# The last q load, its cast and two store flushes moved a dozen letters forward in a hand-written plan (attention, then a token-mixing MLP, one core)

## The chip, the cores and the metric

The kernel runs on one core of a Trainium2 chip. Its engines are TensorE (PE in the profile, with its weight loads as PEld), VectorE (DVE), ScalarE (ACT), GpSimd (POOL) and SyncE (SP, which here only issues DMAs). Each has its own queue and works it off in order; they wait for each other with semaphores. The time is the device time of one execution in microseconds (us). The kernel before took 186.4 us, the median of three runs (185.95 to 187.24); a fourth execution was profiled.

## The reference

There are 8 batches, 12 heads, 448 positions and 64 elements a head. Attention with a sigmoid in place of the softmax gives x (8 x 448 x 768); a MLP then mixes the tokens of each batch with weights that are computed from x itself.

```python
scores = scale * np.matmul(q, k.transpose(0, 1, 3, 2)) - np.log(S)
attn = 1.0 / (1.0 + np.exp(-scores))
x = heads_side_by_side(np.matmul(attn, v))        # 8 x 448 x 768
wq, wk = x @ w_q, x @ w_k                         # 8 x 448 x 64
W_tok = (1 / sqrt(64)) * np.einsum('bsd,btd->bst', wq, wk)
mixed = np.einsum('bst,btd->bsd', W_tok, x)
out = np.maximum(mixed, 0.0) @ w_out
```

## The kernel before

**Tiles.** Work goes by quads: four heads of one batch, 24 quads in all (0 to 23), three to a batch. A quad has seven score steps, each of 64 key positions for four heads. Matmuls work on 64 x 64 quarters of the array, four side by side. PSUM's eight banks are used as four pairs (numbers 0 to 3); which pair a step takes is written out in a string of digits, and a step waits until whoever reads that pair has done so.

**The plan.** The order of all work is a string, PLAN, with a letter for each step; small and capital letters of a kind differ in the engine that copies the result out of PSUM. A loop (L828) walks it and issues each step's instructions to the queues, so the string fixes the order on every engine. The letters around the change:

- S: four score products (L316) into a pair of banks, then the sigmoid on ACT (L332), which frees the pair. S number n belongs to quad n // 7.
- P and p: four products of the sigmoid's result with v (L346). The seventh of a quad is followed by the copy of x out of PSUM, "xt" (L356), which frees the pair.
- c and d: DVE's transposes (L272) of a quad's q and k from its cast tile into the tile "qk" that S reads. They need the tile as GpSimd has arranged it.
- L and l: the wq/wk products of one batch (L406), six letters to a batch. Behind the sixth, DVE adds the two halves (L414, L415) and GpSimd copies wq into a second tile (L420); for the last batch, number 7, DVE does that copy, so GpSimd's last one is that of batch 6.
- N: the transposes of wk (L445, run as L124). x and X: transposes of x (L376). U: L458, the product "tmp" out of wkn and xn. M and m: mixing (L486), which reads the copied wq. O and o: a quarter of an output product (L590). The fourth copies the result to a tile o (L604) and puts a store on a list.
- D: flush(1) (L881, L523). It takes the oldest store off the list and issues its two DMAs on SP.

**Loads.** q, k and v are loaded on SP in a fixed order, ORDER (L703), into six buffers used in turn. pump_loads (L724) runs at every letter and issues the next load as soon as the load six before it has been cast in program order. Two loads have a further condition in BEHIND: `("q", 23): (2642, 2276)` says that the load is put into SP's queue only once more than 2642 products have been issued, and that, in the queue, it waits for product number 2276. pump (L768) runs right after and issues casts in ORDER's order, each as soon as its load has been issued and its target tile is free.

**The cast and the arrangement.** cast1 (L207) puts a quad's q and k, on GpSimd, into one bf16 tile (L212). Once both are there, arrange (L160) follows on GpSimd in the same breath: one copy to a swap tile (L167), two (L170) and two more (L173) that exchange blocks of 32 rows. So a q cast brings five more GpSimd instructions behind it.

Around the change the plan reads, in two pieces with the batch-6 L and l letters in the middle:

```text
... S O L S c l l L S L L S D o d O D S O N x O P S p c p d p D ...
```

Counting the products along it, the first L begins at product 2582, the c stands at 2590, the last L issues products 2610 to 2613 and with them GpSimd's wq copy. The first D comes at 2618, the second at 2642. The O that follows the next S is the first letter at which more than 2642 products have been issued (2646): there the load of q 23, its cast and its arrangement are issued. On GpSimd's queue they stand behind the wq copy. Five stores are on the list at the first L; the two that the two D letters take are output stores of 128 rows by 768 that L657 issues, two DMAs each.

Of the kernel before, what the change touches and what calls it, by code (L numbers as in the profile page):

```python
# [17 lines left out]
def kernel(  # L18
# [111 lines left out]
    def xt(u, j):  # L130
# [14 lines left out]
        "xDSPpPxSPpPDSuwcWwdSSMWOoSMSDwwOOSDxpPSPrPSmPpPDooNDSDSosoOz"  # L145
        "oSDDSxOOSUDpSDPPPDSPpcDSPoDODSSSodOoOSPMpSPPPSPPSwWwoScMSdOw"
        "wSSWOONSPMPcpSPPPPSSOodXSOSxoSoxSOppSpcUPSPpPSoOSdSxOOSPPPmp"
        "pPSPoSoMmOSOLScllLSLLSDodODSONxOPSpcpdpDPSPSPoOSoSOSOoSUSoSO"
        "SpPPpp1SoSOpSPOSOyppPMpPpplMlmlxlLlxOoONooUoOMmooOmooOoOOOOO"
        "oOOOOooOo"  # L150
    )
# [557 lines left out]
    )  # L709
    BEHIND = {("q", 23): (2642, 2276), ("v", 23): (2732, 2404)}  # L710
    BY = {"s": [], "v": []}
    for x in ORDER.split():
        if x[0] == ".":
# [10 lines left out]
    def pump_loads():  # L724
        while len(loaded) < len(ORDER):
            nm, n = ORDER[len(loaded)]
            if len(ring) >= 6 and ring[-6] not in cast:
                break
            emit, m = BEHIND.get((nm, n), (0, 0))
            if emit >= len(products):  # L730
# [204 lines left out]
```

## Time and profile before

| what | value |
|---|---|
| median of three runs | 186.4 us (185.95, 186.4, 187.24) |
| the profiled execution's own time | 186.12 us |
| its span, first to last instruction | 184.3 us |
| PE busy | 171.8 us (93% of the span) |
| ACT busy | 159.6 us (87%) |
| DVE busy | 134.7 us (73%) |
| GpSimd busy | 116.9 us (63%) |
| DMA | 48.50 MB, mean 263 GB/s |

The page's span is 1.8 us shorter than the execution's own time; that part lies before the first and after the last instruction. The shares are means over the whole span and say little on one place: the kernel has a start of some 30 us in which loads and casts set the pace, a long middle in which PE is nearly always busy, and an end in which only output products are left. How the parts hang together is read from the chain of waits (the chain that ended last, followed backwards) and from the timeline, which lists instructions in order of time: start, duration, engine, line, operation, and in brackets the idle time before it with what ended it. In the timeline, runs of equal instructions are merged ("x12") and a row of SP gives the time in which its queue was issuing DMAs.

### The profile page before, as it was taken

The page shows a single profiled execution, that of the slowest core. Times are in us where ns is not written, and L with a number is a line of the kernel's source. Part 1 is how long each engine was busy: PE and PEld are TensorE (multiplying, and loading weights), DVE is VectorE, ACT ScalarE, POOL GpSimd, SP SyncE. Part 2 cuts the span into 40 slices and gives each one's busy share as a digit, 9 for nine tenths or more (in the row PEclk, how much of TensorE's full clock was granted, in tenths as well). Part 3 has the DMA queues.
Part 4 walks back from the last instruction along what each step waited for, and adds up shares of the span by engine and source line. Part 5 has one row for each costly group of instructions (what it writes and reads, how often), then busy time and mean ns, then how long its engine had stood idle before and what let it go on. Part 6 is the DMA issues. An engine that isn't in the chain of part 4 may idle for free.

```text
span 184.3 us, 8238 instructions
## 1 busy us (share of the span) xinstructions
PE 171.8 (93%) x3533; PEld 113.1 (61%) x3534; DVE 134.7 (73%) x207; ACT 159.6 (87%) x207; POOL 116.9 (63%) x156
## 2 busy tenths in 40 slices
PE   7888889899999999999999999999999987999990
PEld 7545435444564555655555556546788886889970
DVE  2457699978998898988758886689786845695310
ACT  4699999999999999999999999889989896984330
POOL 1238787998899995699999919999993270000000
PEclk9999999999999999999999999999999999999999
DMA  5998999969998859999799999997875332442686
GB/s 175 343 386 266 347 377 402 377 215 320 377 396 331 285 193 273 323 320 365 264 240 321 343 305 305 294 403 275 263 212 175 92 88 65 111 92 71 145 219 170
DMA packets 24260, 48.50 MB, mean 263 GB/s; under 512 B 3872, under 2 KB 16416, under 8 KB 24224
## 3 DMA queue, kind: packets, MB, share of 16 engines
q1 hardware_dynamic: 24000, 47.69, 78.3%
q8 instruction: 27, 0.44, 0.9%
q10 hardware_dynamic: 224, 0.30, 0.5%
q14 instruction: 9, 0.07, 0.1%
HBM read 35.78 MB, written 11.01 MB: 254 GB/s over the span
## 4 chain that ended last, share of the span: by engine, by line
PE 78%; DVE 8%; ACT 6%; issue 3%; POOL 2%; DMA 2%; SPq 0%; DVEq 0%; ACTq 0%
PE banks L121 73%; ACT at L332 5%; PE banks L124 4%; DVE qk L252 2%; DVE xt L356 2%; DMA ld<-in_moe_w_k_dram 2%; DVE qk L265 1%; DVE mx L470 1%; POOL wqk L759 1%; POOL qk L212 1%; DVE k L222 1%; DVE xn L385 0%; DVE qk L272 0%; DVE wqk L430 0%; ACT qk L806 0%
## 5 line engine op out<-in xcount | busy, mean ns | idle before, releaser
L332 ACT ACTIVATE at<-banks 128x896 bf16<-128x896 f32 x168 | 141.3, 944 | 7.5 <-PE banks L121 6.9
L121 PE MATMUL banks<-qk 64*64 64x448 bf16 x672 | 61.1, 361 | 5.0 <-ACT at L332 2.5
L121 PE MATMUL banks<-wout,mx 64*64 64x384 bf16 (+2 forms) x816 | 65.4, 324 | 0.1
L212 POOL CAST qk<-ld 128x896 bf16<-128x896 f32 x38 | 44.7, 1194 | 8.4 <-issue 7.4
L121 PEld LDWEIGHTS <-mx 64*64 64x64 bf16 (+2 forms) x816 | 39.1, 105 | 16.4 <-issue 6.0
L121 PE MATMUL banks<-at,v 64*64 64x448 bf16 x672 | 46.8, 350 | 0.3 <-ACT at L332 0.2
L121 PEld LDWEIGHTS <-qk 64*64 64x64 bf16 x672 | 26.5, 105 | 27.0 <-issue 19.4
L356 DVE CAST xt<-banks 128x896 bf16<-128x896 f32 x23 | 24.9, 1084 | 7.7 <-PE banks L121 5.8
L121 PEld LDWEIGHTS <-v 64*64 64x64 bf16 x672 | 23.1, 106 | 6.1 <-issue 1.1
L470 DVE TENSOR_SCALAR mx<-banks 128x896 bf16<-128x896 f32 (+1 forms) x21 | 19.9, 956 | 5.8 <-PE banks L121 5.1
L222 POOL CAST v<-ld 128x896 bf16<-128x896 f32 x22 | 20.4, 934 | 1.2 <-DMA ld<-in_v_dram 0.9
L272 DVE STREAM_TRANSPOSE qk<-qk 128x448 f32<-128x448 f32 x26 | 16.0, 630 | 2.7 <-POOL qk L173 2.6
L385 DVE COPY xn<-banks 128x896 bf16<-128x896 bf16 x21 | 13.1, 624 | 3.8 <-PE banks L124 3.4
L252 DVE STREAM_TRANSPOSE qk<-qk 32x448 f32<-32x448 f32 x24 | 15.3, 636 | 0.6
L170 POOL COPY qk<-qk 32x448 uint32<-32x448 uint32 x26 | 14.4, 554 | 1.6
L173 POOL COPY qk<-swap 32x448 uint32<-32x448 uint32 x26 | 14.4, 554 | 1.5
L121 PE MATMUL banks<-xt,wqk 64*64 64x448 bf16 (+1 forms) x84 | 13.8, 353 | 0.2 <-ACT at L332 0.2
L651 DVE COPY o<-banks 128x384 f32<-128x384 f32 x17 | 9.4, 553 | 3.4 <-PE banks L121 3.0
L124 PEld LDWEIGHTS <-xt 64*64 64x64 bf16 (+1 forms) x588 | 9.8, 108 | 3.2 <-issue 1.8
L124 PE MATMUL banks<-ident,xt 64*64 64x64 bf16 (+1 forms) x588 | 10.4, 194 | 0.2
L121 PE MATMUL banks<-wqk,tmp 64*64 64x448 bf16 (+3 forms) x72 | 8.5, 291 | 0.0
L121 PE MATMUL banks<-wq,tmp 64*64 64x448 bf16 (+2 forms) x72 | 8.4, 292 | 0.0
(68 smaller groups left out, 136.7 us busy)
## 6 DMA issues: line engine op xcount, KB each, us to landing
ld<-in_q_dram SPq DMA_DIRECT2D x24, 448.0 KB, 5.8
ld<-in_v_dram SPq DMA_DIRECT2D x24, 448.0 KB, 5.7
ld<-in_k_dram SPq DMA_DIRECT2D x23, 448.0 KB, 5.5
out_dram<-o SPq DMA_DIRECT2D x38, 192.0 KB, 5.0
out_dram<-ld SPq DMA_DIRECT2D x14, 192.0 KB, 2.8
ld<-in_moe_w_out_dram SPq DMA_DIRECT2D x6, 384.0 KB, 5.1
wout<-wout SPq DMA_DIRECT2D x6, 192.0 KB, 5.7
out_dram<-o SPq DMA_DIRECT2D x4, 96.0 KB, 1.9
```

Source lines behind the costliest of these rows:

```text
L121: products.append(nc.tensor.matmul(*args, **kw))
L124: products.append(nc.tensor.transpose(*args, **kw))
L170: eng.tensor_copy(out=w[lo, 1], in_=w[hi, 0])
L173: eng.tensor_copy(out=w[hi, 0], in_=z[lo])
L212: COPY[e](out=f[:, :, "qk".index(nm)].rearrange("p e i d y -> p e y i d"), in_=ld.pop((nm, n)).rearrange("p (y i e d) -> p e y i d", y=2, ...
L222: COPY[e](out=t16.rearrange("p i b d -> p b i d"), in_=ld.pop((nm, n)).rearrange("p b (i d) -> p b i d", i=NI),)
L252: nc.vector.transpose(out=qk[n][other : other + 32, h].rearrange("p t i n -> p (t i n)").bitcast(F32), in_=w[own : own + 32, 1 - h],)
L272: nc.vector.transpose(out=qk[n][:, t].rearrange("p t i n -> p (t i n)").bitcast(F32), in_=w)
L332: nc.scalar.activation(dst, src, ACTF.Sigmoid, bias=attn_bias, scale=attn_scale)
L356: COPY[eng](out=xt(u, j), in_=ps)
L385: COPY[eng](out=xn, in_=ps)
L470: nc.vector.tensor_scalar(dst, ps, moe_scale, 0.0, ALU.mult, ALU.max)
```

## The change

The two letters D that stood behind the last L letters of batch 6 now stand in front of the c. The condition under which the load of q 23 is issued falls from "more than 2642 products" to "more than 2590 products"; the product that the load waits for in SP's queue, 2276, stays. With the new number the load is issued at the second l behind the c, where 2594 products have been issued, and the cast of q 23 with its arrangement at the same letter. On GpSimd's queue these six instructions now come ahead of the wq copy of batch 6, which is issued with the last L. No instruction is added or removed.

```diff
-        "pPSPoSoMmOSOLScllLSLLSDodODSONxOPSpcpdpDPSPSPoOSoSOSOoSUSoSO"
+        "pPSPoSoMmOSOLSDDcllLSLLSodOSONxOPSpcpdpDPSPSPoOSoSOSOoSUSoSO"
...
-    BEHIND = {("q", 23): (2642, 2276), ("v", 23): (2732, 2404)}
+    BEHIND = {("q", 23): (2590, 2276), ("v", 23): (2732, 2404)}
```

## The prediction

> **What bounds the kernel now.** I read the page's busy shares first, then the chain that ended last, then, at the one place where the chain leaves PE near the change, the timeline by engine. The busy shares and the granted clock:
>
> ```profile
> PE 171.8 (93%) x3533; PEld 113.1 (61%) x3534; DVE 134.7 (73%) x207; ACT 159.6 (87%) x207; POOL 116.9 (63%) x156
> PEclk9999999999999999999999999999999999999999
> ```
>
> PE is busy for 93% of the span at full clock, so over most of it only a PE pause is worth anything. The chain in order of time, late part:
>
> ```profile
> 146.89 4.73 PE banks L121 x106
> 151.62 0.03 DVEq L604
> 151.65 0.60 DVE qk L272
> 152.25 0.99 DVE xt L356
> 153.24 0.04 issue
> 153.28 7.71 PE banks L121 x186
> ...
> 166.46 13.48 PE banks L121 x310
> ```
>
> From 146.89 to the last output products near 179.95 the chain is on PE, but for one detour over DVE between 151.62 and 153.28: a transpose (L272), then the copy of x (L356). The timeline shows PE there:
>
> ```profile
> 148.85 0.41 PE L121 MATMUL banks<-at,v 64*64 64x448 bf16 x4
> ...
> 150.69 0.41 PE L121 MATMUL banks<-qk 64*64 64x448 bf16 x4
> 150.88 0.71 PE L121 MATMUL banks<-wout,mx 64*64 64x384 bf16 x12
> ...
> 153.28 0.38 PE L121 MATMUL banks<-qk 64*64 64x448 bf16 x4 [1.68 <-DVE xt L356]
> ```
>
> The products at 153.28 are score step S159. Its banks are pair 1, which held the x of quad 21 and comes free with the copy xt. That x was complete with the four v products at 148.85, so near 149.26. Why the copy came three microseconds later stands in DVE's rows:
>
> ```profile
> 147.58 0.95 DVE L604 COPY o<-banks 128x768 f32<-128x768 f32 x1
> 151.08 1.17 DVE L272 STREAM_TRANSPOSE qk<-qk 128x448 f32<-128x448 f32 x2 [2.55 <-POOL qk L173]
> 152.17 1.05 DVE L356 CAST xt<-banks 128x896 bf16<-128x896 f32 x1
> 153.15 0.94 DVE L604 COPY o<-banks 128x768 f32<-128x768 f32 x1
> ```
>
> DVE was free at 148.53 and stood 2.55 us at the two transposes of quad 23 (c, d), which stand ahead of xt in its queue and wait for GpSimd's last L173 copy. S159 doesn't need them: it belongs to quad 22. GpSimd's rows give the cause:
>
> ```profile
> 138.65 1.20 POOL L212 CAST qk<-ld 128x896 bf16<-128x896 f32 x1
> 146.15 0.56 POOL L420 COPY wq<-wqk 64x448 bf16<-64x448 bf16 x1 [6.31 <-ACT at L332]
> 146.77 1.20 POOL L212 CAST qk<-ld 128x896 bf16<-128x896 f32 x1
> 148.03 0.56 POOL L167 COPY swap<-qk 128x448 uint32<-128x448 uint32 x1
> 148.66 1.17 POOL L170 COPY qk<-qk 32x448 uint32<-32x448 uint32 x2
> 149.88 1.17 POOL L173 COPY qk<-swap 32x448 uint32<-32x448 uint32 x2
> ```
>
> After the cast of k 23 (138.65 to 139.85) GpSimd idles 6.31 us at the wq copy, which needs DVE's sum (L415). The page names ACT as the releaser; the row that fits is this one, ending at 145.99:
>
> ```profile
> 145.37 0.62 DVE L415 TENSOR_TENSOR wqk<-banks,wpart 128x448 bf16<-128x448 f32 x1
> ```
>
> Behind the copy stand the cast of q 23 and its arrangement, 146.77 to 151.05. So GpSimd's order, not its speed, makes the pause: it waits idle with work behind it.
>
> **The change part by part.** SP's queue and the load, in the views of SP and of the DMA issues:
>
> ```profile
> 127.00 4.73 SPq L657 DMA_DIRECT2D out_dram<-o  x6
> 132.50 0.33 SPq L190 DMA_DIRECT2D ld<-in_q_dram  x1
> 134.29 1.31 SPq L612 DMA_DIRECT2D out_dram<-o  x2
> ld<-in_q_dram SPq DMA_DIRECT2D x1, 448.0 KB, 4.6
> ```
>
> Six L657 DMAs are three stores: one forced out by the tile allocation at the O before the first L, and those of the two D. Then comes q 23's load. After the change the two D still take the same two stores (the list holds five there) and still stand ahead of the load. So SP's order doesn't change at all: 0 us. Were the D not moved, the load would pass two stores. The load is issued at 132.50 as before, and lands 4.6 us later, at 137.1.
>
> GpSimd: the cast of q 23 now follows that of k 23, 139.85. The load has been there for 2.75 us; the cast's tile is that of k 23, already being written. The five instructions with their gaps take what they took, 151.05 - 146.77 = 4.28 us: from about 139.90 to 144.18. The wq copy is then next and starts at 146.15 as before, as its input comes at 145.99; the cover is 1.97 us. Without that cover a late copy costs nothing at first either: its readers are the mixing products of batch 6,
>
> ```profile
> 161.69 0.27 PE L121 MATMUL banks<-wq,tmp 64*64 64x256 bf16 x2
> ```
>
> some 15 us behind the copy. Nothing else stands behind it on GpSimd.
>
> DVE: the transposes start when it is free, 148.53 + 0.02 = 148.55, and end 1.17 later, 149.72. xt, complete in PSUM at 149.26, runs 149.72 to 150.77. The o copy of 153.15 needs the products of 150.88, which end at 151.59: it runs about 151.64 to 152.58.
>
> PE: steps follow in a fixed rhythm; S at 150.69, O at 150.88, the next S would start as much later as S follows O everywhere here:
>
> ```profile
> 150.02 0.41 PE L121 MATMUL banks<-qk 64*64 64x448 bf16 x4
> 150.21 0.71 PE L121 MATMUL banks<-wout,mx 64*64 64x384 bf16 x12
> ```
>
> that is 150.69 - 150.21 = 0.48, so S159 could start at 150.88 + 0.49 = 151.37. Pair 1 is free at 150.77 + 0.06 (the 0.06 is xt's end, 153.22, to the products at 153.28). So S159 starts 153.28 - 151.37 = 1.91 us earlier. The view of waits counts only 1.68, because it begins the pause at the modelled end of the last product, 151.59. I take 1.91, since starts are recorded and ends modelled; 1.68 stays as the lower end.
>
> What is late next? ACT:
>
> ```profile
> 147.85 4.41 ACT L332 ACTIVATE at<-banks 128x896 bf16<-128x896 f32 x5 [0.86 <-PE banks L121]
> ...
> 153.71 0.92 ACT L332 ACTIVATE at<-banks 128x896 bf16<-128x896 f32 x1 [1.45 <-PE banks L121]
> 154.93 6.62 ACT L332 ACTIVATE at<-banks 128x896 bf16<-128x896 f32 x8 [0.31 <-PE banks L121]
> ```
>
> ACT is busy until 152.26 and idled 1.45 + 0.31 = 1.76 us afterwards; its eight sigmoids in a row take 6.62, 0.81 apart. After the change those of S159 and S160 close up: S159's directly behind the run of five, whose last one started 0.92 before its end, so at 151.34 + 0.81 = 152.15; S160's (products at 154.44 - 1.91 = 152.53, ended 152.92) near 153.0, against 154.93. That is 1.93 earlier, so ACT follows. If a sigmoid closes up only at its full 0.92 rather than at the pace, S160's starts at 152.26 + 0.92 = 153.18, 1.75 earlier.
>
> PE's next products, and what they wait for:
>
> ```profile
> 154.44 0.39 PE L121 MATMUL banks<-qk 64*64 64x448 bf16 x4
> 154.63 0.77 PE L121 MATMUL banks<-xn,wkn 64*64 64x192 bf16 x28
> 155.21 0.39 PE L121 MATMUL banks<-qk 64*64 64x448 bf16 x4
> ```
>
> S160 at 152.53 takes the banks of S158, whose sigmoid ends by 152.26. The U products at 154.63 - 1.91 = 152.72 take pair 0, free with the o copy at 152.58 + 0.06 = 152.64: 0.08 us to spare, the tightest place. S161 at 153.30 takes pair 1 from S159's sigmoid, which ends near 153.1; it is the first step that reads quad 23, whose transposes are long done. Behind that each wait is for work that itself moves: the x copies, the last wq/wk sum, stores issued as results come. Everything that doesn't move (the loads of q 23 and v 23) is over by then. So the gain stands to the end.
>
> Two bounds of unknown cost remain. GpSimd's 4.28 us move beside other DVE work (140.28 to 144.5). If GpSimd slowed DVE, the transpose at 143.90 ahead of L414 and L415 would be hit, and the wk transposes on PE (N) need L415's result. The nearest rows, one with GpSimd busy in L173 and one with it idle:
>
> ```profile
> 136.54 1.17 POOL L173 COPY qk<-swap 32x448 uint32<-32x448 uint32 x2
> 136.62 0.64 DVE L272 STREAM_TRANSPOSE qk<-qk 128x448 f32<-128x448 f32 x1
> ...
> 143.90 0.63 DVE L272 STREAM_TRANSPOSE qk<-qk 128x448 f32<-128x448 f32 x1
> ```
>
> 0.64 against 0.63: I take 0, and as the upper end one L173 copy, 1.17 / 2 = 0.58 us. Below nothing it can be only by the 0.01 that separates the two o copies above (0.95 with GpSimd busy, 0.94 without).
>
> The Trainium skill, page "SBUF — State Buffer", section "Who interferes with whom", speaks of a port that VectorE and GpSimd share, locked for a whole instruction when VectorE runs in a two-port mode: the other then stands still. By that lock DVE would lose up to the 0.58 above and the gain would be 1.3; the same section says that an instruction with at most one SBUF input outside those modes doesn't contend, and the two rows above, 0.64 and 0.63, agree with this for the transposes.
>
> The sum against the profiled execution: span 184.3 - 1.9 = 182.4, time 186.12 - 1.9 = 184.2. That execution lies 0.28 below the median shown; from the median it is 184.5. I take the middle of the four times shown (186.12 and 186.4 are the inner two, mean 186.26): 184.4.
>
> **The rivals.** (1) Part of the gain is lost at the next wait: ACT's closing up, the 0.08 us at the U products, or DVE stopped behind one L173 copy. For it: ACT is 87% busy and its spare time here, 1.76, is about the gain. Against: starts worked out above leave each a margin. By ACT's 1.75 the time is 184.5; by the stopped DVE, 1.91 - 0.58 = 1.33, it is 184.9.
>
> (2) The change doesn't do what it says: q 23's load lands so late that the transposes wait as before. GpSimd now needs it at 139.9 and ended 6.87 us sooner (144.18 for 151.05); the transposes come later than 148.55 only if it lands after 139.9 + 4.37 = 144.3, and as late as before only at 146.8, against 137.1 seen. For it: nothing in the rows but a DMA load that could vary. Time 186.3.
>
> (3) Slower: without the pause PE runs unbroken from before 146 to the end, and the granted clock falls. The remaining 26.7 us of PE (153.28 to 179.95) give back 1.91 at a clock of 26.7 / 28.6 = 0.93, from there on it is slower; at 0.90 they take 29.7, and the time is 186.26 - 1.91 + 3.0 = 187.3. Against: the clock row has a 9 in all slices, long unbroken stretches among them.
>
> **How the numbers follow.** The whole gain (1.7 to 2.1) gets 0.79, rival 1 beyond that (0.5 to 1.6) 0.12, rival 2 0.05, rival 3 0.04. The range takes in rival 1 with its stopped DVE and the spread of the runs shown: below, the lowest run less the largest gain, 185.95 - 2.1, and some 0.2 for one more chip's spread, 183.6; above, the median less 0.7, 185.7. About 1% is what a measurement of this kernel can tell from no change, and 1% of 186.4 is 1.86, against 1.91 forecast: the forecast lies on that line. Of the 0.79 a little over half, with runs that fall well, goes to faster, 0.49; the rest of it, rivals 1 and 2 make 0.47 for within 1%; slower 0.04.
>
> **What would show it.** GpSimd: the L212 cast near 139.9, L173 ended by 144.2, L420 still near 146.15 and now last. DVE: L272 x2 near 148.55 without its 2.55 us, xt at 149.7. PE: no wait for xt, S159 near 151.4. ACT: one run of 14 sigmoids from 147.85 with no 1.45 in it. SP: same order. Span near 182.4. Wrong it would be if the cast still waited after 139.9, if DVE's rows of 140 to 146 stretched, or if PE paused anew between 152.5 and 161.

## The result, and the profile after

The changed kernel takes 184.88 us (median of nine runs, 183.92 to 185.28); the kernel before, in the nine runs then known, 186.4 us. The ratio of the two is 0.9909, 95% interval 0.988 to 0.9939: by 1.1 to 2.2 us faster. The execution that was profiled took 185.28 us, its span is 183.5 us (before: 186.12 and 184.3).

GpSimd's rows of the timeline after (start, duration, engine, line, operation, idle time before it):

```profile
138.78 0.93 POOL L222 CAST v<-ld 128x896 bf16<-128x896 f32 x1
139.66 2.30 POOL L212 CAST qk<-ld 128x896 bf16<-128x896 f32 x2
142.02 0.56 POOL L167 COPY swap<-qk 128x448 uint32<-128x448 uint32 x1
142.65 1.17 POOL L170 COPY qk<-qk 32x448 uint32<-32x448 uint32 x2
143.87 1.17 POOL L173 COPY qk<-swap 32x448 uint32<-32x448 uint32 x2
147.15 0.56 POOL L420 COPY wq<-wqk 64x448 bf16<-64x448 bf16 x1 [2.11 <-ACT at L332]
```

The two casts of quad 23 now stand together, the arrangement follows, and the wq copy comes last. It still waits, 2.11 us for 6.31, but nothing is behind it. Every row of this part lies 1.00 us later than before (the k 23 cast at 139.66 for 138.65, the wq copy at 147.15 for 146.15); that offset is not of the change, as the experiments show. On the clock of the first profile the arrangement ends at 145.04 - 1.00 = 144.04.

DVE's and PE's rows of the same timeline:

```profile
148.58 0.95 DVE L604 COPY o<-banks 128x768 f32<-128x768 f32 x1
149.44 1.16 DVE L272 STREAM_TRANSPOSE qk<-qk 128x448 f32<-128x448 f32 x2
150.53 1.05 DVE L356 CAST xt<-banks 128x896 bf16<-128x896 f32 x1
152.70 0.96 DVE L604 COPY o<-banks 128x768 f32<-128x768 f32 x1 [1.12 <-ACT at L332]
```

```profile
151.70 0.41 PE L121 MATMUL banks<-qk 64*64 64x448 bf16 x4
151.89 0.71 PE L121 MATMUL banks<-wout,mx 64*64 64x384 bf16 x12
152.37 0.41 PE L121 MATMUL banks<-qk 64*64 64x448 bf16 x4
152.56 1.20 PE L121 MATMUL banks<-wout,mx 64*64 64x384 bf16 x24
153.54 0.41 PE L121 MATMUL banks<-qk 64*64 64x448 bf16 x4
153.73 0.80 PE L121 MATMUL banks<-xn,wkn 64*64 64x192 bf16 x28
```

The bracket of 2.55 us at DVE's transposes is gone, xt follows at once, and the score step S159 comes at 152.37 without a bracket, 0.48 us behind the products in front of it. Less the offset that is 151.37, for 153.28 before: 1.91 us earlier. ACT's row is one unbroken run of 14 sigmoids, where before there were five, one and eight:

```profile
148.85 11.82 ACT L332 ACTIVATE at<-banks 128x896 bf16<-128x896 f32 x14 [0.86 <-PE banks L121]
```

The chain that ended last, in order of time, no longer leaves PE at this place:

```profile
147.89 12.22 PE banks L121 x292
...
165.59 13.48 PE banks L121 x310
```

Of the 1.91 us the profiled span shows only 184.3 - 183.5 = 0.8; it is 183.5 where some 182.4 was forecast. The rest went to the start-up. An early and a later cast of GpSimd, before and after:

```profile
12.97 0.94 POOL L222 CAST q<-ld 128x896 bf16<-128x896 f32 x1 [2.75 <-DMA ld<-in_q_dram]
...
70.98 2.30 POOL L212 CAST qk<-ld 128x896 bf16<-128x896 f32 x2 [1.80 <-issue]
```

```profile
14.79 0.94 POOL L222 CAST q<-ld 128x896 bf16<-128x896 f32 x1 [4.30 <-DMA ld<-in_q_dram]
...
71.99 2.31 POOL L212 CAST qk<-ld 128x896 bf16<-128x896 f32 x2 [2.34 <-issue]
```

An early q load landed later, and at 71 us, with equal queues up to there, the second execution is 1.0 us behind. The 1.82 us of that cast are not what is passed on: in the first repeat below it comes at 12.50, earlier than before, and that execution is 0.85 us behind all the same. From 71 us on both run in step up to the changed place. Whether this belonged to the change had to be tested.

### The profile page after: what moved, and what is told of

Its sections match the earlier page's. It is cut to its first block, busy times and chain, and to the rows that moved or that the text cites. A ratio compares the mean times of both kernels' runs of the same rounds, so it can differ in the third digit from the quotient of the medians.

```text
span 183.5 us, 8238 instructions
## 1 busy us (share of the span) xinstructions
PE 171.1 (93%) x3534; PEld 112.7 (61%) x3534; DVE 134.5 (73%) x207; ACT 159.7 (87%) x207; POOL 116.7 (64%) x156
## 4 chain that ended last, share of the span: by engine, by line
PE 75%; ACT 8%; DMA 7%; DVE 5%; issue 1%; POOL 1%; ACTq 0%; POOLq 0%
PE banks L121 71%; ACT at L332 8%; DMA ld<-in_q_dram 7%; PE banks L124 4%; DVE xt L356 1%; DVE mx L470 1%; DVE qk L252 1%; DVE xn L385 1%; DVE qk L265 1%; POOL q L222 1%; DVE wqk L430 0%; ACT q L791 0%; DVE ld L558 0%; ACT ld L558 0%; DVE wkn L450 0%
## 5 line engine op out<-in xcount | busy, mean ns | idle before, releaser
L173 POOL COPY qk<-swap 32x448 uint32<-32x448 uint32 x26 | 14.4, 555 | 1.5
```

The lines of the kernel that those rows point to most:

```text
L173: eng.tensor_copy(out=w[hi, 0], in_=z[lo])
```

## The experiments

A span mixes the start-up with the changed place, so each profile is also read by three instants: the score step S154 (the last one ahead of the work in question), S159 (the one that stood), and the last store's issue on SP (L562). Times are those of the profiles' timelines, in us; the ratios are against the kernel before on the same chip.

| kernel | S154 at | S154 to S159 | S159 to last issue | median | ratio, 95% interval |
|---|---|---|---|---|---|
| before | 147.34 | 5.94 | 27.43 | 186.4 | |
| after | 148.34 | 4.03 | 27.46 | 184.88 | 0.9909 (0.988 to 0.9939) |
| e1_again | 148.19 | 4.03 | 27.46 | 184.81 | 0.9913 (0.9879 to 0.9946) |
| e2_flush_only | 147.54 | 5.94 | 27.43 | 186.28 | 0.9992 (0.9966 to 1.0019) |
| e3_load_only | 147.71 | 4.03 | 27.45 | 184.54 | 0.9898 (0.9867 to 0.9929) |
| e4_wq_dve | 148.44 | 4.04 | 27.45 | 184.14 | 0.9887 (0.9856 to 0.9918) |
| e5_xt_first | 147.00 | 4.03 | 27.83 | 184.89 | 0.9931 (0.9898 to 0.9965) |
| e6_load_139 | 147.37 | 4.03 | 27.46 | 184.19 | 0.9884 (0.9849 to 0.9918) |
| e7_load_142 | 147.75 | 4.83 | 27.42 | 185.9 | 0.9979 (0.9955 to 1.0004) |
| e8_again | 147.19 | 4.03 | 27.45 | 184.11 | 0.9901 (0.9872 to 0.993) |
| e9_load_only | 148.81 | 4.04 | 27.45 | 184.66 | 0.9916 (0.9884 to 0.9947) |
| e10_load_139 | 148.20 | 4.03 | 27.45 | 184.87 | 0.9931 (0.9906 to 0.9955) |

**The changed kernel again.** No edit.

> The changed kernel once more, as the measure for the other runs on this chip. My theory: the whole pause of PE in front of S159 is gone and nothing comes in its place, so from the cast of k 23 on (138.65 before) everything behind S159 runs 1.91 us earlier, the end included: 1.9 us faster, ratio 0.990. Rival (start-up): the profiled execution after the change was only 0.8 us shorter in its span because something before the changed place got 1.0 us slower by the change itself; then the cast of k 23 comes near 139.7 again here, and not in a profile with the queues of before. Rival (part lost later): the distance from S159 to the last instruction grows.

S154 comes 0.85 us later than in the profile of before, but S154 to S159 is again 4.03 for 5.94, and from S159 to the end 27.46 for 27.43. The gain behind S154 is 1.91 - 0.03 = 1.88 us, and nothing of it is lost later. The ratio's interval holds the expected 0.990. That the slow start-up showed in this profile too left the start-up rival open; it is taken up at the end.

**Only the flushes.**

```diff
-        "...SOLScllLSLLSDodODSONxOP..."
+        "...SOLSDDcllLSLLSodOSONxOP..."
     BEHIND = {("q", 23): (2642, 2276), ...}
```

> The kernel before with the two D moved and the load condition left at 2642. The five queues hold the same instructions in the same order as before, as the two stores are the next ones in SP's queue either way. My theory: no change, ratio 1.000, pause of 1.7 us before S159 as before. It shows what two equal sets of queues differ by, at the start-up too. Rival (the stores matter): stores issued earlier free their tiles sooner, and part of the 1.9 us shows here.

As my theory has it: 0.9992, and the pause is there as before.

```profile
153.48 0.38 PE L121 MATMUL banks<-qk 64*64 64x448 bf16 x4 [1.68 <-DVE xt L356]
```

Moving the two D alone changes no engine's queue and no time.

**Only the load's condition.**

```diff
-    BEHIND = {("q", 23): (2642, 2276), ("v", 23): (2732, 2404)}
+    BEHIND = {("q", 23): (2590, 2276), ("v", 23): (2732, 2404)}
```

> The kernel before with only the load condition changed to 2590; the two D stay. GpSimd's order becomes that of the changed kernel, and on SP the q 23 load passes two stores (four DMAs, about 3.3 us of issue time). My theory: GpSimd's order is all that counts; the stores are issued some 0.4 us later and nobody waits for their tiles, so the gain is the same 1.9 us, ratio 0.990, as in the changed kernel. Rival (the flushes are needed): the delayed stores hold a tile or the v 23 load, and 0.5 us or more of the gain is missing.

S154 to S159 is 4.03, ratio 0.9898: the whole gain, with two stores behind the load instead of ahead of it. So the number 2590 does everything, through GpSimd's order; the moved flushes only keep SP's order as it was, and here that order has no price that can be seen.

**The wq copy on DVE, all else as before.**

```diff
-                (nc.vector if tail else nc.gpsimd).tensor_copy(out=w2[HALF[1], span], in_=w[HALF[0], span])
+                (nc.vector if tail or u == NU - 2 else nc.gpsimd).tensor_copy(out=w2[HALF[1], span], in_=w[HALF[0], span])
```

> The kernel before with one instruction on another engine: the wq copy of batch 6 runs on DVE instead of GpSimd. SP and the order of the loads stay as before. My theory (GpSimd stood idle at that copy with the cast behind it): the q 23 cast follows the k 23 cast at once, the arrangement ends near 144.2, and S159 starts 1.9 us earlier; DVE pays about 0.27 us for the copy near 146, where PE has the wk transposes ahead of it, so 1.7 to 1.9 us faster, ratio 0.990 to 0.991. Rival (the load came late, or its place in the program counts): the cast still waits after 140 and the pause stays, ratio 1.000.

With the copy out of GpSimd's queue the two casts stand together, although the load and its cast are issued at the old letter:

```profile
139.78 2.30 POOL L212 CAST qk<-ld 128x896 bf16<-128x896 f32 x2
142.14 0.56 POOL L167 COPY swap<-qk 128x448 uint32<-128x448 uint32 x1
...
147.12 0.27 DVE L420 COPY wq<-wqk 64x448 bf16<-64x448 bf16 x1
```

S154 to S159 is 4.04 and the ratio 0.9887. The rival falls: the load was there, and GpSimd stood at the wq copy. DVE's 0.27 us cost PE nothing that can be told: the second profile of the load-only kernel (e9), without that copy on DVE, has 4.04 too.

**xt ahead of the transposes on DVE, GpSimd as before.**

```diff
-        "...SONxOPSpcpdpDPSPSPoOSoSO..."
+        "...SONxOPSpppDPSPSPcdoOSoSO..."
```

> The kernel before with the two letters c and d of quad 23 moved behind the last P of quad 21: on DVE the copy xt comes ahead of the two transposes; GpSimd, PE, ACT and SP as before. My theory: S159 needs xt and not the transposes, so it starts 1.9 us earlier although GpSimd still ends at 151.05. The transposes then run from 151.1 to 152.25 and the o copy behind them to about 153.2 instead of 152.6, and the U products wait for its banks: a new pause of some 0.5 us, so 1.4 us faster, ratio 0.9925. Rival (quad 23's tile itself is the bound): no gain, ratio 1.000.

```profile
149.04 1.09 DVE L356 CAST xt<-banks 128x896 bf16<-128x896 f32 x1 [0.86 <-PE banks L121]
150.73 1.17 DVE L272 STREAM_TRANSPOSE qk<-qk 128x448 f32<-128x448 f32 x2 [0.59 <-POOL qk L173]
151.82 0.92 DVE L604 COPY o<-banks 128x768 f32<-128x768 f32 x1
...
152.80 0.77 PE L121 MATMUL banks<-xn,wkn 64*64 64x192 bf16 x28 [0.18 <-DVE o L604]
```

The transposes wait for GpSimd as late as before, and S159 comes all the same after 4.03 us. So quad 23's tile was never what S159 needed; its transposes only stood ahead of xt. DVE's order is thus as much a part of the cause as GpSimd's: the pause needed both. The new wait is where it was expected, at the U products behind the o copy. It costs 27.83 - 27.43 = 0.40 us against 0.5 expected, and leaves 1.91 - 0.40 = 1.51 (ratio 0.9931). The bracket shows only 0.18, 0.22 less, for the same reason for which the 1.68 fell short of 1.91.

**The load held back, by two amounts.**

```diff
-    BEHIND = {("q", 23): (2590, 2276), ("v", 23): (2732, 2404)}
+    BEHIND = {("q", 23): (2590, 2495), ("v", 23): (2732, 2404)}    # and 2568
```

> The changed kernel with the q 23 load made to wait in SP's queue for product 2495 instead of 2276, so that it is issued near 139.5 instead of 132.5 (on the clock of the first profile) and lands 3 to 4.6 us later, 142.5 to 144.1. My theory: the cast then starts with the landing, the arrangement ends between 146.8 and 148.4, still ahead of DVE's 148.55, and the wq copy comes up to 2.8 us later than before, where its readers leave 15 us: the whole gain stays, 1.9 us, ratio 0.990. Rival (the wq copy's lateness or the load's slack counts): 0.5 us or more is lost.

> The changed kernel with the q 23 load made to wait for product 2568, issued near 142.3 and landing at 145.3 to 146.9. My theory: cast and arrangement end 4.28 us behind the landing, at 149.6 to 151.2; the transposes come that late, then xt (1.17 + 1.05 us later), and S159 starts at 151.9 to 153.5 instead of 151.4: between 0.5 us of the gain lost and all of it, ratio 0.993 to 1.000, with S159 starting 6.5 to 6.6 us behind the landing. Rival: as in the run before it nothing is lost, as S159 doesn't read that tile.

GpSimd in the first and the second of them:

```profile
143.69 1.19 POOL L212 CAST qk<-ld 128x896 bf16<-128x896 f32 x1 [3.84 <-DMA ld<-in_q_dram]
...
146.79 1.17 POOL L173 COPY qk<-swap 32x448 uint32<-32x448 uint32 x2
148.02 0.55 POOL L420 COPY wq<-wqk 64x448 bf16<-64x448 bf16 x1
```

```profile
146.06 1.21 POOL L212 CAST qk<-ld 128x896 bf16<-128x896 f32 x1 [5.87 <-DMA ld<-in_q_dram]
...
149.18 1.17 POOL L173 COPY qk<-swap 32x448 uint32<-32x448 uint32 x2
150.40 0.55 POOL L420 COPY wq<-wqk 64x448 bf16<-64x448 bf16 x1
```

In the first the cast waits 3.84 us for the landing and the wq copy runs 1.8 us later than before (148.02 for 146.15, with 0.03 off for the start-up); the gain is whole (4.03, ratio 0.9884). In the second the arrangement ends at 150.35, and S159 comes at 152.58, 6.52 us behind the cast's start, inside the expected 6.5 to 6.6. DVE's rows show the way there:

```profile
150.38 1.17 DVE L272 STREAM_TRANSPOSE qk<-qk 128x448 f32<-128x448 f32 x2 [1.32 <-POOL qk L173]
151.47 1.05 DVE L356 CAST xt<-banks 128x896 bf16<-128x896 f32 x1
```

S158 is also late in that profile, by 0.43 us (see the last section), but xt ends at 152.52, 0.06 us ahead of S159, so it is xt that S159 waits for. In that profile 0.8 us of the gain is lost; over its ten runs most of it is (0.9979, interval up to 1.0004). That profile's execution, 185.42 us, was among the fastest of the ten; I take the landing to vary from run to run, but only one execution was profiled, so this stays open.

**The start-up rival.** After nine and six runs the changed kernel lay somewhat above kernels with the same PE, DVE and ACT queues. So it ran beside them once more, with no new edit.

> The changed kernel a third time, beside the next two, whose PE, DVE and ACT queues are the same and which differ from it only in how SP issues the last q load. So far the changed kernel's runs lie more often near 185.1 than those of the two others (medians 184.9 against 184.5 and 184.2), and in its two profiles the score step S154 came 0.85 to 1.0 us later than in the first profile of before, while the stretch behind S154 was 1.87 us shorter. My theory: the start-up varies from run to run by about 1.4 us with the landing of the first loads, whatever the kernel, and 15 runs happened to fall badly: the three medians agree within 0.3 us now, near 0.990. Rival: the changed kernel has the slower start-up more often for a reason of its own: its median lies 0.4 us or more above both others again.

> The kernel before with only the load condition changed to 2590, again. My theory: S154 to S159 takes 4.03 us as in the changed kernel, ratio 0.990, median within 0.3 us of the changed kernel's in the same call. Rival: 0.4 us or more below it.

> The changed kernel with the q 23 load waiting for product 2495, again. My theory: S154 to S159 takes 4.03 us, ratio 0.990, median within 0.3 us of the changed kernel's in the same call. Rival: 0.4 us or more below it.

The order turned round: 184.11 for the changed kernel, 184.66 and 184.87 for the others. The rival falls. My "within 0.3 us" was too narrow, however: medians of 6 to 12 runs of kernels with equal stretches behind S154 differ by up to 0.76 us. The profiles say the same: in eleven of the twelve the offset that S154 has against the first profile is already there, within 0.01 us, at GpSimd's cast near 71 us, more than 50 us ahead of the first instruction that any of these edits moves. In the twelfth (e3) 0.18 us more comes between the two. The 21 runs of the changed kernel together have a median of 184.56.

## Why the prediction was right

**GpSimd's order, passed on by DVE's, is the cause: shown.** Three different edits (the load's condition alone, the wq copy on another engine, xt ahead on DVE) each remove the pause before S159, and the flushes alone don't. The predicted places, with 1.00 us taken off the profile after: arrangement ended at 144.18, measured 144.04; wq copy 146.15, measured 146.15; transposes 148.55, measured 148.44; xt 149.72, measured 149.53. The last two came 0.1 to 0.2 us earlier because neighbouring DVE rows overlap: the o copy runs to 149.53, the transposes begin at 149.44.

**Start to start, not the bracket.** S159 was forecast at 151.37 and came at 151.37; the pause was worth 1.91 us, and the 1.68 of the view of waits was too low because it counts from a modelled end: the row of products at 150.88 is given 0.71 us, while the next S follows such a row after 0.48. Both ends had been kept; the choice was right.

**What was late next: nothing.** ACT closed up as worked out, in one run of 14. S160 was forecast at 152.53 and came at 152.54, the U products at 152.72 and 152.73. The tightest place, those products behind the o copy, was identified rightly: in the xt-first kernel, where that copy is later, it is the one that costs. It was tighter than forecast: the o copy ended at 153.66 - 1.00 = 152.66, not 152.58, so with the 0.06 us that the prediction counts from a copy's end to the products only 0.01 us was to spare, not 0.08. From S159 to the end the loss is 0.03 us.

**SP and the flushes: no price.** SP's queue is the same before and after, and the load-only kernel shows that even the other order is free.

**The rivals.** GpSimd slowing DVE: GpSimd was idle from 139.85 to 146.15 before; now it works nearly without a break from 139.66 to 145.04, and the DVE rows beside it take what they took (1.09, 1.09, 0.96 and 0.63 before), each 1.00 to 1.01 us later. So the 0.58 us of the bound weren't there:

```profile
141.28 1.09 DVE L356 CAST xt<-banks 128x896 bf16<-128x896 f32 x1 [0.94 <-PE banks L121]
142.76 1.09 DVE L470 TENSOR_SCALAR mx<-banks 128x896 bf16<-128x896 f32 x1 [0.38 <-PE banks L121]
144.03 0.96 DVE L604 COPY o<-banks 128x768 f32<-128x768 f32 x1 [0.18 <-PE banks L121]
144.90 0.64 DVE L272 STREAM_TRANSPOSE qk<-qk 128x448 f32<-128x448 f32 x1
```

The transpose of 144.90 runs beside the last L173 copy for 0.14 us only; for a transpose wholly beside one the prediction's pair of 0.64 and 0.63 is the evidence.

A late load: not in any profile of the changed kernel, and the held-back loads show the point where it would decide. In e10 the cast came at 144.68 - 0.86 = 143.82 on the clock of the first profile and nothing was lost, in e7 at 146.06 - 0.41 = 145.65 and 0.8 us was; the forecast was 144.3. The cast in e10:

```profile
144.68 1.20 POOL L212 CAST qk<-ld 128x896 bf16<-128x896 f32 x1 [4.00 <-DMA ld<-in_q_dram]
```

A falling clock: the page after shows the granted clock as before in all 40 slices, its mean is 0.998, and the stretch from S159 to the end takes 27.46 for 27.43.

```profile
PEclk9999999999999999999999999999999999999999
```

**What was mis-sized** is the scatter around the sum. The prediction gave 184.4; the median was 184.88, and 184.56 over all 21 runs. The sum of the change stands (1.88 us behind S154 in the first repeat), but the time of S154 itself goes from 147.00 to 148.81 over twelve profiles whose queues are the same up to some 127 us, and nearly all of that is there by 71 us. The prediction allowed some 0.2 us for such spread at the lower end and didn't look for its source. With it, the side of the 1% line on which a 1.91 us gain is measured is left to chance: 0.9909 came out just within 1%, to which the prediction gave 0.47, against 0.49 for faster. Whether the last 0.2 us between the ratio (0.9909, or 1.7 us of 186.4) and the 1.88 us is scatter alone isn't separated; every interval of the changed kernel holds 1.88.

## What to carry to other kernels

When PE waits for a copy, look at what stands ahead of that copy in its engine's queue: here the wait was passed on through two in-order queues from an instruction that PE's next product had no use for. An instruction that waits long with ready work behind it is worth reordering even on an engine that is 63% busy, and here GpSimd's order or another engine for one copy each gave the whole gain, and DVE's order 1.51 us of it. Price a PE pause by the starts of products on both sides and the rhythm around it, and compare executions by stretches between fixed instructions, since a start-up that varies by nearly as much as the gain hides it in the spans.

## What the runs showed of the hardware that was not expected

The start-up varies by 1.8 us (S154 at 147.00 to 148.81) with the same instructions in the same queues. From GpSimd's cast near 71 us on the offset stays as it is within 0.01 us, but for one profile of twelve (e3), in which 0.18 us is added; why is open.

In the kernel with the load held back to product 2568, stores and two loads come close together, and PE pauses with no releaser that the profile shows:

```profile
147.00:149.00 2.00, 2.00 (x78) 1.88 (x63) 1.82 (x3) 1.14 (x2) 1.82 (x4) 1.00 1.03 324
149.00:151.00 2.00, 2.00 (x47) 1.29 (x39) 0.68 (x3) 1.92 (x4) 1.78 (x4) 1.00 0.95 316
...
151.21 0.65 PE L121 MATMUL banks<-wout,mx 64*64 64x384 bf16 x9 [0.20 <-issue]
151.21 0.27 PEld L121 LDWEIGHTS <-mx 64*64 64x64 bf16 x8 [0.60 <-issue]
```

The first two rows are of the table by stretches (PE, PEld, DVE, ACT and GpSimd busy, granted clock 1.00, DMA share, GB/s), for the time up to the pause; in the profile of before, DMA moved 0 and 166 GB/s in them. S158, behind the pause, starts 1.10 us after S157, for 0.67 before. A DMA share nearly as high came without a pause elsewhere: in e10 0.97 at 302 GB/s from 145 to 147 us, with PE busy throughout. The cause was not tested.
